# Causal attention with decay and an MLP mixer: scores computed a second time in transposed layout, with the maximum as an operand row

## The chip, the cores and the metric

The kernel runs on one core of a Trainium2 chip. The metric is the device time of one execution in microseconds. Before: median of 3 runs 1118.24 us (1116.69 to 1120.88).

## The reference

8 batches of 8 heads, 576 positions, head dimension 64. The outputs of all heads of a batch, 576 x 512, then go through a token mixing and a channel mixing layer, with a residual in each.

```python
scores = scale * np.matmul(q, k.transpose(0, 1, 3, 2))
log_f = np.log(np.clip(f, 0.0001, 1.0))
cum = np.cumsum(log_f, axis=-1)
decay = cum[:, :, :, None] - cum[:, :, None, :]
scores = np.where(causal, -1000000000.0, scores + decay)
scores = scores - np.max(scores, axis=-1, keepdims=True)
attn = np.exp(scores)
attn = attn / (np.sum(attn, axis=-1, keepdims=True) + 1e-09)
x = np.matmul(attn, v)          # then laid out as batch, position, head * dimension
xt = x.transpose(0, 2, 1)
h = np.maximum(xt @ w_tok1, 0.0) @ w_tok2
u = x + h.transpose(0, 2, 1)
h2 = np.maximum(u @ w_ch1, 0.0) @ w_ch2
return u + h2
```

The weights come in as doubles and are decoded on the chip. Nearly every product is made from two parts: a number is written as hi + lo, both fp32r, and hi x hi, hi x lo and lo x hi are added up in PSUM.

## The kernel before, in words

`build` walks through the 64 heads and records every operation with its engine, duration, reads, writes, buffers and a priority; `Plan.run` then places them, always the ready operation with the lowest priority whose buffers are free, and this fixes the order on each engine's queue. The priority is the head's number plus offsets from tables (`OFF`, `STEP`, `HEAD` and others). All DMAs stand on SyncE's queue, in that order.

A head, in tiles of queries with 64, 128, 128, 128, 128 rows (t = 0 to 4). For a pair of heads q and k are loaded into `raw` and split into `hl` (hi on GpSimd, lo on GpSimd); three gathers of 288 KB each (line 834) bring hi and lo of one head into the operands `k1` and `k2`, and two small DMAs bring the cumulated decay into rows of `k2`. `score` (line 861) multiplies in two passes, `k1` and `k2`, queries on the PSUM partitions; `rmin` (868, VectorE) adds the mask and takes the minimum of the negated row; `expo` (875, ScalarE) writes the exponentials to SBUF (`pr`) and their sums, which a second instruction reads out; lines 893 and 896 form the reciprocal; `norm` (903, GpSimd) multiplies the five tiles. Then 15 transposes of 128 x 128 (917, TensorE, fp32) bring the probabilities to keys on partitions, ScalarE and VectorE copy them out as hi and lo (585, 594), GpSimd moves a lo part (588), and the values are the weights of up to 512 moving columns of probabilities (lines 987 to 999): 11 matmuls, the result with dimensions on partitions. ScalarE and VectorE add hi and lo sums into `xt` (1037, 1044, 1047). Heads 0 to 3 (`FQ`, `FV`) skip the splitting: they multiply fp32 data directly.

After 4 and after 8 heads of a batch, `mixer` runs for half of the channels: `trx` transposes x (1416, 10 transposes), `tok1` and `tok2` mix the tokens, 28 matmuls of 256 and 24 of 288 columns; `tok2` adds the residual on VectorE (1487). After the second half `ch1` and `ch2` do two of twelve blocks of the channel layer (96 matmuls of 288 columns). u and the partial sums go to HBM.

When all heads are done, the attention buffers are given up for the other channel weights. Two chunks of 512 positions are done with 10 blocks of the channel layer (480 matmuls of 512 columns), seven with a Strassen scheme (per chunk 210 of 256 and 120 of 512 columns). Before the first score TensorE does 120 small filler matmuls (line 645), in early gaps.

```python
for of, j0, w in segs:
    for x, k in enumerate((at(k2),) if fq else (at(k1), at(k2))):
        nc.tensor.matmul(ps[:m, of : of + w], k[:, 0, i0 : i0 + m], k[:, 1, j0 : j0 + w], start=(x == 0), stop=(fq or x == 1))
...
def tr(out, i, j, pr=pr):
    nc.tensor.transpose(out, at(pr)[:, poff[i] + start[j] : poff[i] + end[j]], E["ident"])
```

Of the kernel before, what the change touches and what calls it, by code (L numbers as in the profile page):

```python
# [15 lines left out]
P = 128  # L16

PRM = dict(
    FILL=120, EP=3, DB=0, DLAST=1, F1=2, FQ=4, FV=4, LAG=3.88, n_raw=1, n_vr=2, n_hl=1, n_k1=2, n_k2=2, n_vv=2,
    E_hi='POOL', E_lo='POOL', E_vh='ACT', E_vl='POOL', E_nrm='POOL', n_pr=3, n_p34=2, n_p2=2, n_p1=1, n_p0=1, n_low=1,  # L20
    n_ring=12, n_part=4, n_xt=2, n_d_raw=3, n_d_g=2, n_hid=3, DEC3=11.96, SPREAD=10.59, SPREADA=6.46,
)
OFF = dict(
    load=-19.94, kh=41.36, kl=82.19, qh=-131.14, ql=-77.18, vh=-106.52, vl=134.93, s4=5.08, s3=5.41, s2=-18.34, mn=9.94,
    ex=6.58, rec=-18.92, nrm=-207.34, t3=4.41, t2=-99.36, t1=-68.13, t0=-31.7, hl=-31.09, av=4.12, fold=-29.94,
    fpe=3.65, lo0=-43.16, fev=-183.41, u=-72.11, dec=73.32, dec2=37.66, dec3=1.32, cd=-18.17, vload=-19.23,
)
# [516 lines left out]
def build(nc, env, dims):  # L544
# [61 lines left out]
    def decay():  # L606
# [6 lines left out]
        def c():  # L613
            return asf(at(cc)[:, 2, :])
# [1141 lines left out]
```

## Time and profile before

| | |
|---|---|
| median of the runs | 1118.24 us |
| the profiled execution | 1112.94 us |
| its span | 1111.2 us |
| busy: TensorE, VectorE, ScalarE, GpSimd | 1069.8, 765.0, 644.0, 546.4 us |
| mean granted clock | 0.991 |
| scores, from the first to the last start (L861) | 13.2 to 585.4 us |

Start and length of a matmul are given in the profile; the length holds the way through the array and overlaps the next, so the distance between two starts in an unbroken row is what one costs. Weight loads (PEld) are instructions of their own beside the matmuls. An fp32 matmul that is not a transpose shows as two records.

### The profile page before, as it was taken

Reading aid. Unit: us, or ns where it says so; the run is one execution under the profiler, and the core shown is the slowest. Engines: PE = TensorE matmul, PEld = TensorE weight load, DVE = VectorE, ACT = ScalarE, POOL = GpSimd, SP = SyncE. Lnnn points to the kernel's source line nnn. Section 1 sums busy time; section 2 is a strip of 40 time slices with the busy share of each in tenths; the row PEclk is TensorE's granted clock in tenths of the full one; section 3 lists DMA queues with packets and bytes.
Section 4 is the critical chain, followed back from the end, with each engine's and each line's share of the span. In section 5 each row is a group of like instructions: output and inputs, shape, how many; then the busy total and the mean of one; then the engine's idle time right before and its main releaser. Section 6 shows DMA issues by size and latency. Waiting matters only on the chain.

```text
span 1111.2 us, 20873 instructions
## 1 busy us (share of the span) xinstructions
PE 1069.8 (96%) x7172; PEld 962.4 (87%) x7172; DVE 765.0 (69%) x1944; ACT 644.0 (58%) x1657; POOL 546.4 (49%) x631
## 2 busy tenths in 40 slices
PE   8998979999999999999999999999999999999998
PEld 5577868999899999889898888889989898989896
DVE  6787878788787777778788896566455554637362
ACT  5776767778788777778776543244242433424241
POOL 5576876778678676777763305703123030303010
PEclk9999999999999999999999999999999999999999
DMA  8577675876777686767762544231212121212011
GB/s 225 144 176 165 158 201 142 217 215 174 202 179 206 177 194 194 185 193 176 181 171 82 184 145 125 68 113 40 76 39 77 38 77 39 76 39 76 16 62 39
DMA packets 69610, 146.79 MB, mean 132 GB/s; under 512 B 9424, under 2 KB 26832, under 8 KB 68480
## 3 DMA queue, kind: packets, MB, share of 16 engines
q1 hardware_dynamic: 69504, 145.45, 47.8%
q8 instruction: 57, 0.93, 0.4%
q14 instruction: 49, 0.40, 0.1%
HBM read 63.46 MB, written 28.31 MB: 83 GB/s over the span
## 4 chain that ended last, share of the span: by engine, by line
PE 75%; DMA 9%; DVE 6%; SPq 3%; ACT 3%; POOL 2%; issue 2%; DVEq 0%; POOLq 0%; ACTq 0%
DMA k<-hl 8%; PE bank L917 6%; PE pair L1364 6%; PE pair L1363 6%; PE pair L1365 6%; PE bank L861 6%; PE bank L1300 5%; PE bank L1302 5%; PE bank L1301 5%; PE pair L861 2%; PE pair L997 2%; PE pair L999 2%; SPq L834 2%; PE bank L1130 2%; PE pair L1151 2%
## 5 line engine op out<-in xcount | busy, mean ns | idle before, releaser
L903 POOL TENSOR_SCALAR pr<-pr,rec 128x576 f32<-128x576 f32 (+4 forms) x320 | 165.9, 539 | 53.9 <-DVE rec L896 33.1
L1334 POOL TENSOR_TENSOR part<-part,xt 128x512 f32<-128x512 f32 x28 | 36.0, 1316 | 277.3 <-DMA part<-pd 205.0
L585 ACT ACTIVATE p<-bank 128x384 fp32r<-128x384 f32 (+3 forms) x300 | 128.4, 474 | 45.2 <-PE bank L917 41.8
L917 PE MATMUL bank<-ident,pr 128*128 128x128 f32 (+1 forms) x960 | 137.9, 277 | 5.7 <-DVE p L594 2.0
L875 ACT ACTIVATE pr<-bank,nmin 128x448 f32<-128x448 f32 (+3 forms) x256 | 118.0, 467 | 36.9 <-DVE nmin L868 35.0
L594 DVE TENSOR_TENSOR p<-bank,p 128x384 fp32r<-128x384 f32 (+1 forms) x180 | 106.4, 595 | 41.0 <-ACT p L585 39.2
L1310 DVE TENSOR_TENSOR dd<-bank,dd 128x256 f32<-128x256 f32 x245 | 98.0, 422 | 52.3 <-PE bank L1302 50.3
L868 DVE CUSTOM_DVE_ANT_0 bank<-bank,mask 128x448 f32<-128x448 f32 (+3 forms) x256 | 107.0, 433 | 29.7 <-PE bank L861 26.1
L917 PEld LDWEIGHTS bank<-ident,pr 128*128 128x128 f32 (+1 forms) x960 | 109.3, 132 | 19.2 <-DVE low L594 3.4
L1363 PE MATMUL pair<-hid,w2r 128*128 128x512 f32 x280 | 109.0, 389 | 0.0
L1364 PE MATMUL pair<-hid,w2r 128*128 128x512 f32 x280 | 109.0, 389 | 0.0
L1365 PE MATMUL pair<-hid,w2r 128*128 128x512 f32 x280 | 108.9, 389 | 0.0
L594 DVE TENSOR_TENSOR hid<-dd,hid 128x512 fp32r<-128x512 f32 x70 | 48.4, 692 | 86.3 <-ACT hid L585 86.3
L861 PE MATMUL bank<-k 128*128 128x320 f32 (+1 forms) x480 | 88.9, 310 | 10.1 <-DMA k<-hl 8.4
L585 ACT ACTIVATE hid<-dd 128x512 fp32r<-128x512 f32 x70 | 44.0, 629 | 89.9 <-PE pair L1364 89.0
L1313 ACT ACTIVATE dd<-dd 128x256 f32<-128x256 f32 x140 | 56.8, 415 | 61.4 <-DVE dd L1310 59.2
L1300 PE MATMUL bank<-ring,w1r 128*128 128x256 f32 x280 | 79.8, 285 | 0.1
L861 PEld LDWEIGHTS bank<-k 128*128 128x128 f32 (+1 forms) x480 | 64.0, 178 | 18.2 <-DMA k<-hl 8.5
L1302 PE MATMUL bank<-ring,w1r 128*128 128x256 f32 x280 | 79.1, 283 | 0.0
L1301 PE MATMUL bank<-ring,w1r 128*128 128x256 f32 x280 | 79.1, 282 | 0.0
L999 PE MATMUL pair<-p,vv 128*128 128x512 f32 x240 | 75.6, 323 | 0.0
L790 POOL TENSOR_TENSOR hl<-raw,hl 128x1152 fp32r<-128x1152 f32 x27 | 72.5, 2684 | 1.8
(152 smaller groups left out, 3250.3 us busy)
## 6 DMA issues: line engine op xcount, KB each, us to landing
k<-hl SPq DMA_DIRECT2D x180, 288.0 KB
raw<-in_qk SPq DMA_DIRECT2D x30, 576.0 KB
vr<-in_v SPq DMA_DIRECT2D x32, 320.0 KB
ud<-xt SPq DMA_DIRECT2D x8, 1152.0 KB
pd<-part SPq DMA_DIRECT2D x32, 288.0 KB
out_t<-part SPq DMA_DIRECT2D x36, 256.0 KB
dd<-in_w_ch SPq DMA_DIRECT2D x12, 512.0 KB
dd<-in_w_ch SPq DMA_DIRECT2D x40, 128.0 KB
```

The lines of the kernel that those rows point to most:

```text
L585: nc.scalar.activation(out, in_, func, scale=scale)
L594: nc.vector.tensor_tensor(out, in_, asf(hi), op=ALU.subtract)
L861: nc.tensor.matmul(ps[:m, of : of + w], k[:, 0, i0 : i0 + m], k[:, 1, j0 : j0 + w], start=(x == 0), stop=(fq or x == 1))
L875: nc.scalar.activation(at(pr)[:m, poff[t] : poff[t] + w], at(buf)[:m, of : of + w], AF.Exp, bias=E["nmin"][sm][:m, t : t + 1], scale=-1.0, ...
L903: nc.gpsimd.tensor_scalar(x, x, r, 0.0, op0=ALU.mult, op1=ALU.add)
L917: nc.tensor.transpose(out, at(pr)[:, poff[i] + start[j] : poff[i] + end[j]], E["ident"])
L1300: nc.tensor.matmul(q, wh[:, cs], h_, start=c == 0, stop=False)
L1301: nc.tensor.matmul(q, wl[:, cs], h_, start=False, stop=False)
L1302: nc.tensor.matmul(q, wh[:, cs], l_, start=False, stop=c == 1)
L1363: nc.tensor.matmul(q, wh, h_, start=x == 0, stop=False)
L1364: nc.tensor.matmul(q, wl, h_, start=False, stop=False)
L1365: nc.tensor.matmul(q, wh, l_, start=False, stop=x == F2 - 1)
```

## The change

Scores are multiplied twice. First, with the hi parts only, queries on partitions (`ascore`, five tiles in six matmuls): VectorE takes the maximum of each row (`mx`). A transpose of the five columns of maxima, a ScalarE copy with factor -1 (`mt`) and a DMA of 2560 bytes put them as a row into `k2` (`md`). Then the scores are multiplied again in both terms with keys on the partitions (`bscore`), the maximum being subtracted by that row. ScalarE takes the exponential in place in PSUM, VectorE clamps what lies beyond the diagonal by a minimum with `tri`, and hi and lo parts are copied to `pp`. There is no normalizing before the values, and no transpose of probabilities.

The probabilities are now the weights, 128 (for the last tile 64) columns, and v is the moving operand: lo, hi and two columns of ones in 130 columns for the hi part, 66 for the lo part, so that the sum of a row comes out as a column. 15 pairs of tiles, two matmuls each, with tokens on the partitions. ScalarE and VectorE add the two sums, GpSimd multiplies by the reciprocal (`nx`), and hi and lo parts go to `xn`, which `tok1` reads; `trx` is gone. In `tok2` the residual is added on TensorE by matmuls with `xn` as weights and an identity as moving operand (11 for each of 4 channel blocks and batch), and ScalarE copies the result out, where VectorE added before. The fp32 path of the first four heads is gone. `k2` has three buffers, not two. Priorities come from a table `PR` with a value for each single operation, in place of the offsets; the plan's other rules are as before.

```diff
-    FILL=120, EP=3, DB=0, DLAST=1, F1=2, FQ=4, FV=4, LAG=3.88, n_raw=1, n_vr=2, n_hl=1, n_k1=2, n_k2=2, n_vv=2,
+    FILL=120, EP=3, DB=0, F1=2, n_raw=1, n_vr=1, n_hl=1, n_k1=2, n_k2=3, n_vv=2, n_pp=5, n_tm=1, n_xs=2, n_mt=3,
...
+            pr_("kh", n), lambda k2=k2, f=gather: f(at(k2)[0:D, T0:].rearrange("p (a s) -> p a s", a=2), 0, 2),
+        dma(pr_("kl", n), lambda k1=k1, f=gather: f(at(k1)[0:D], 0, 3), 294912, dur=650, rate=220, rd=[(hl, 0), (hl, 1)], wr=[(k1, 0)], bufs=[k1, hl])
+        dma(pr_("kl", n, 0.01), lambda k1=k1, f=gather: f(at(k1)[D:P], 1, 2), 294912, dur=650, rate=220, rd=[(hl, 0), (hl, 1)], wr=[(k1, 1)], bufs=[k1, hl])
...
+        def ascore(t, where=where, k2=k2):
+            buf, segs = where[t]
+            i0 = T0 + end[t] - P
+            for of, j0, w in segs:
+                nc.tensor.matmul(at(buf)[:, of : of + w], at(k2)[: D + 2, i0 : i0 + P], at(k2)[: D + 2, PADQ + j0 : PADQ + j0 + w], start=True, stop=True)
...
+            nc.vector.tensor_tensor_reduce(x, x, E["mask"][:, S - w : S], 1.0, -3e38, op0=ALU.add, op1=ALU.max, accum_out=E["mx"][sm][:, t : t + 1])
...
+            "PE", [tp_(P, NS)], pr_("mt", n), lambda um=um, sm=sm: nc.tensor.transpose(at(um)[:NS, :P], E["mx"][sm], E["ident"]),
...
+        dma(pr_("md", n), lambda mt=mt, k2=k2: nc.sync.dma_start(asf(at(k2)[D + 2 : D + 3, :PADQ]), asf(at(mt))), 2560, dur=650, rd=[mt, "rows"], wr=[(k2, "m")], bufs=[mt, k2])
...
+            def bscore(u=u, ps=ps, k1=k1, k2=k2):
+                segs = [(512 - HS, 0, 0, HS), (512, 0, HS, HS)] if u == "c" else [(of, j, kst[j], kw[j]) for j, of in UNITS[u]]
+                for of, j, q0, w in segs:
+                    o_, a, m = at(ps)[: ksz[j], of : of + w], kst[j], ksz[j]
+                    nc.tensor.matmul(o_, at(k1)[:, 1, a : a + m], at(k1)[:, 0, q0 : q0 + w], start=True, stop=False)
+                    nc.tensor.matmul(o_, at(k2)[: D + 3, PADQ + a : PADQ + a + m], at(k2)[: D + 3, T0 + q0 : T0 + q0 + w], start=False, stop=True)
...
+            p.op("ACT", d_act(w_), pr_("ex" + u, n), lambda f=region: nc.scalar.activation(f(), f(), AF.Exp, scale=1.0 / D**0.5), wr=[ps], bufs=[ps])
...
+                nc.vector.tensor_tensor(x, x, y, op=ALU.min)
...
+            p.op("ACT", d_act(w_), pr_("hi" + u, n), lambda f=region, pb=pb, w_=w_: hi_act(at(pb)[:, 0, :w_], f()), rd=[ps], wr=[(pb, 0)], bufs=[ps, pb])
+            p.op("DVE", d_dve(w_), pr_("lo" + u, n), lambda f=region, pb=pb, w_=w_: lo_dve(at(pb)[:, 1, :w_], f(), at(pb)[:, 0, :w_]), rd=[ps, (pb, 0)], wr=[(pb, 1)], bufs=[ps, pb])
...
+        def avt(ts, av=av, vv=vv, v0=v0, pp=pp):
+            for t in ts:
+                m = ksz[t]
+                for j in range(t + 1):
+                    u, of = AT_[j]
+                    c0 = of + P * (t - j)
+                    for z in (0, 1):
+                        w = at(pp[u])[: ksz[j], z, c0 : c0 + m]
+                        a, c = (T0, 2 * D + 2) if z else (0, 2 * D + 2)
+                        nc.tensor.matmul(
+                            at(av)[:m, AVS * t + a : AVS * t + c], w, at(vv)[: ksz[j], v0 + j, a:c], start=(j == 0 and z == 0), stop=(j == t and z == 1)
+                        )
...
+        p.op(ENG["ev"], d_act(NS * D), pr_("ev", n), lambda A=A, tm=tm: hi_on(ENG["ev"], at(tm), A()[:, :, 0:D]), rd=avs, wr=[tm], bufs=[av, tm])
...
+        p.op("DVE", d_dve(NS * D), pr_("xs", n), lambda A=A, tm=tm, xs=xs: nc.vector.tensor_tensor(at(xs), A()[:, :, D : 2 * D], at(tm), op=ALU.add), rd=[*avs, tm], wr=[xs], bufs=[av, tm, xs])
+        p.op("POOL", d_ptt(NS * D), pr_("nx", n), lambda xs=xs, sm=sm: nc.gpsimd.tensor_tensor(at(xs), at(xs), rec(sm).unsqueeze(2).to_broadcast([P, NS, D]), op=ALU.mult), rd=[("rec", sm)], wr=[xs], bufs=[xs])
...
+        p.op(ENG["xh"], d_hi(ENG["xh"], NS * D), pr_("xh", n), lambda xn=xn, xs=xs, hc=hc: hi_on(ENG["xh"], at(xn)[:, :NS, hc], at(xs)), rd=[xs], wr=[(xn, h, 0)], bufs=[xn, xs])
+        p.op("POOL", d_ptt((NS - 1) * D), pr_("xl", n), lambda xn=xn, xs=xs, hc=hc: lo_pool(at(xn)[:, NS:, hc], at(xs)[:, : NS - 1], at(xn)[:, : NS - 1, hc]), rd=[xs, (xn, h, 0)], wr=[(xn, h, 1)], bufs=[xn, xs])
...
-            def trs(ps=ps, blocks=blocks, w=w, first=g == (2,), tr=tr):
-                for x, (i, j) in enumerate(blocks):
-                    tr(at(ps)[:, x * P : (x + 1) * P], i, j)
...
-        def norm(t, sm=sm, pr=pr):
-            m = size[t]
-            x = at(pr)[:m, poff[t] : poff[t] + end[t]]
...
-        def av0(av=av, vv=vv, v0=v0, pb=p0_, fv=fv, vr=vr):
-            x, w_, r_ = (at(av)[:D], at(vr)[:T0, v0, :], at(pb)[:T0]) if fv else (at(av), at(vv)[:, v0, :], at(pb))
-            nc.tensor.matmul(x[:, 512:1024], w_, r_[:, T0:], start=True, stop=False)
-            nc.tensor.matmul(x[:, off : off + T0], w_, r_[:, :T0], start=True, stop=True)
...
-        def avj(seq, pb, av=av, vv=vv, v0=v0, fv=fv, vr=vr):
-            for j, c0, z in seq:
-                w, last = S - start[j], (j, z) == (3, 0)
-                x = at(av)[:, off + start[j] : off + S]
-                if fv:
-                    nc.tensor.matmul(x[:D], at(vr)[:, v0 + j, :], at(pb)[:, c0 : c0 + w], start=False, stop=last)
-                elif z:
-                    nc.tensor.matmul(x[:D], at(vv)[:, v0 + j, :D], at(pb)[:, 1, c0 : c0 + w], start=False, stop=last)
-                else:
-                    nc.tensor.matmul(x, at(vv)[:, v0 + j, :], at(pb)[:, 0, c0 : c0 + w], start=False, stop=last)
-
...
-    def trx(g):
...
-                            at(ps)[:m, i * W + c * P : i * W + (c + 1) * P], at(xt)[:, part * HC + c, start[t] : end[t]], E["ident"]
...
+                    if k == NT - 1:
+                        for t, z, a, e_ in own_x:
+                            eye = E["eyes"] if t == NS - 1 else E["eye"][:, a - t * P : e_ - t * P]
+                            nc.tensor.matmul(at(ps)[:, a - hf * HS : e_ - hf * HS], at(xn)[:, t + NS * z, ds], eye, start=False, stop=False)
```

In the middle of the attention stage, on TensorE, stood before: transposes of probabilities (`pr`) between scores (`k`) and values (`p`, `vv`).

```order
L917 MATMUL bank_68<-ident,pr_156 128x128 x4
L861 MATMUL bank_66<-k_149 128x320
L861 MATMUL bank_66<-k_151 128x320
L861 MATMUL bank_66<-k_149 128x192
L861 MATMUL bank_66<-k_151 128x192
L917 MATMUL bank_65<-ident,pr_156 64x128 x4
L997 MATMUL pair_64<-p_159,vv_152 64x384
L999 MATMUL pair_64<-p_159,vv_152 128x384
```

Now it reads, at a like place, with `pp` the probabilities and `vv` the values:

```order
L761 MATMUL pair_64<-vv_165,pp_170 128x130
L761 MATMUL pair_64<-vv_165,pp_170 128x66
L761 MATMUL pair_64<-vv_165,pp_167 128x130
L761 MATMUL pair_64<-vv_165,pp_167 128x66
L761 MATMUL pair_64<-vv_165,pp_167 128x130
L761 MATMUL pair_64<-vv_165,pp_167 128x66
L761 MATMUL pair_64<-vv_165,pp_168 64x130
L761 MATMUL pair_64<-vv_165,pp_168 64x66
L761 MATMUL pair_64<-vv_165,pp_170 64x130
L761 MATMUL pair_64<-vv_165,pp_170 64x66
L761 MATMUL pair_64<-vv_165,pp_167 64x130
L761 MATMUL pair_64<-vv_165,pp_167 64x66
```

The transposes are gone, and each value matmul has weights of its own and few columns.

In `tok2` one block of the mixer stood on TensorE as six matmuls:

```order
L1473 MATMUL bank_67<-held,ring_129 128x288
L1474 MATMUL bank_67<-held,ring_129 128x288
L1475 MATMUL bank_67<-held,ring_130 128x288
L1473 MATMUL bank_67<-held,ring_129 128x288
L1474 MATMUL bank_67<-held,ring_129 128x288
L1475 MATMUL bank_67<-held,ring_130 128x288
```

Now, with `x` the split outputs and `eye` the identity:

```order
L1177 MATMUL bank_65<-held,ring_134 128x288
L1182 MATMUL bank_65<-held,ring_134 128x288
L1183 MATMUL bank_65<-held,ring_135 128x288
L1177 MATMUL bank_65<-held,ring_134 128x288
L1181 MATMUL bank_65<-eye,x_133 128x128 x4
L1181 MATMUL bank_65<-eye,x_133 128x32 x2
L1182 MATMUL bank_65<-held,ring_134 128x288
L1183 MATMUL bank_65<-held,ring_135 128x288
```

Six matmuls with new weights stand among them.

On SyncE, in the middle of the attention stage, before, with `hl` the split inputs, `cc` the decay, `ud` the store of u:

```order
L810 DMA vr_146<-in_v 128x640
L828 DMA k_151<-cc_164 2x1x576 x2
L834 DMA k_148<-hl_147 64x2x576
L834 DMA k_148<-hl_147 64x1152
L834 DMA k_151<-hl_147 64x2x576
L1498 DMA ud_102<-xt_122 128x2304
L828 DMA k_150<-cc_164 2x1x576 x2
L810 DMA vr_145<-in_v 128x640
```

Now, with `mt` the maxima:

```order
L658 DMA k_160<-cc_175 2x1x576
L664 DMA k_158<-hl_156 64x2x576
L664 DMA k_158<-hl_156 64x1152
L710 DMA k_161<-mt_162 1x5x128
L1210 DMA ud_112<-x_132 128x2304
L710 DMA k_159<-mt_162 1x5x128
L664 DMA k_160<-hl_156 64x2x576
L664 DMA k_161<-hl_156 64x2x576
L658 DMA k_161<-cc_175 2x1x576
L664 DMA k_157<-hl_156 64x2x576
```

The transfer of the maxima stands in order with the gathers and the stores.

More of the change, by code (lines that the diff above doesn't have):

```diff
@@ L552, in build @@
     end = [a + b for a, b in zip(start, size)]
-    poff = [sum(end[:t]) for t in range(NS)]
     F2 = NF - F1
     p = Plan()
-    LAG, FQ, FV = PRM["LAG"], PRM["FQ"], PRM["FV"]
     def mm_(n, m=P):
@@ L719, in go @@
             def go(prio):
-                if t == 0:
-                    loads = [(sl(r * T0, T0), sl(0, DT), w_tok1[0:T0, :]) for r in (0, 1)]
+                if t == NS - 1:
+                    loads = [(sl(r * T0, T0), sl(0, DT), w_tok1[P * t :, :]) for r in (0, 1)]
                 else:
-                    loads = [(full, sl(0, DT), w_tok1[start[t] : end[t], :])]
+                    loads = [(full, sl(0, DT), w_tok1[P * t : P * t + P, :])]
                 decode(prio, loads, DT, lambda: E["t1h"][:, t, :], lambda: E["t1l"][:, t, :], ("t1", t))
@@ L907, in build @@
-        p.op("DVE", 72, n + o["rec"], rec1, rd=[("sums", sm, t) for t in range(NS)], wr=[("rec", sm)])
-        p.op("DVE", 100, n + o["rec"], rec2, wr=[("rec", sm)])
-        for t in (4, 3, 2, 1, 0):
-            p.op(ENG_NRM, d_pts(end[t], 1) if ENG_NRM == "POOL" else d_dve(end[t], True), n + o["nrm"], lambda t=t, f=norm: f(t), rd=[("rec", sm)], wr=[(pr, t)], bufs=[pr])
-        p34, p2_, p1_, p0_ = (Buf(("f" if fv else "p") + x) for x in ("34", "2", "1", "0"))
-        low = Buf("low")
-        def tr(out, i, j, pr=pr):
-            nc.tensor.transpose(out, at(pr)[:, poff[i] + start[j] : poff[i] + end[j]], E["ident"])
@@ new lines, in A, with rec @@
+        def A(av=av):
+            return at(av)[:, : AVS * NS].rearrange("p (t c) -> p t c", t=NS)
+        def rec(r):
+            return E["rec"][r]
+        avs = [(av, x) for x in range(3)]
+        p.op(ENG["ev"], d_act(NS * D), pr_("ev", n), lambda A=A, tm=tm: hi_on(ENG["ev"], at(tm), A()[:, :, 0:D]), rd=avs, wr=[tm], bufs=[av, tm])
+        p.op("DVE", 76, pr_("rc", n), lambda A=A, sm=sm: nc.vector.tensor_scalar(rec(sm), A()[:, :, 2 * D], 1e-9, None, op0=ALU.add), rd=avs, wr=[("rec", sm)], bufs=[av])
@@ L1433, in mixer @@
+    if "u" not in st:
+        st["u"], st["xt"] = {}, Buf("ux")
+    u, xt = st["u"], st["xt"]
+    heads = [(xn, h, z) for h in range(part * H // 2, (part + 1) * H // 2) for z in range(3)]
     h1 = []
@@ L1635, in attn_mixer_kernel @@
     )
-    for nm, shape in (("nmin", [P, NS]), ("sums", [P, NS + 1]), ("rec", [P, NS // 2 + 1, 4])):
-        E[nm] = [const.tile(shape, F32, name=f"{nm}{i}") for i in range(4)]
-    for x in E["sums"]:
-        nc.vector.memset(x, 1.0)
+    tri = E["tri"] = const.tile([P, P + 64], F32, name="tri")
+    nc.gpsimd.memset(tri, 3e38)
+    for a, w in ((0, 64), (64, P)):
+        nc.gpsimd.affine_select(
+            out=tri[:, a : a + w], in_=tri[:, a : a + w], pattern=[[1, w]], compare_op=ALU.is_ge, fill=0.0, base=0, channel_multiplier=-1
+        )
+    eye = E["eye"] = const.tile([P, P], F32R, name="eye")
+    eyes = E["eyes"] = const.tile([P, 64], F32R, name="eyes")
+    nc.vector.tensor_copy(eye, ident)
+    for a in (0, 64):
+        nc.vector.tensor_copy(eyes[a : a + 64], ident[a : a + 64, a : a + 64])
+    for nm in ("mx", "rec"):
+        E[nm] = [const.tile([P, S // P + 1], F32, name=f"{nm}{i}") for i in range(4)]
+    for x in E["mx"]:
+        nc.vector.memset(x, 0.0)
+    for x in E["one"].values():
+        nc.vector.memset(x[64:, :64], 0.0)
+    nc.vector.memset(pairs[1][64:, 704:834], 0.0)
     E["lower"] = const.tile([P, 1], F32, name="lower")
```

749 lines of the change are left out of this document (322 added, 427 removed), and 192 rows, old and new, of tables (av, cd, ex, fold).

## Prediction

> **What bounds the kernel now.** I read the busy times and the chain on the page first, then busy times by stage.
>
> ```profile
> span 1111.2 us, 20873 instructions
> PE 1069.8 (96%) x7172; PEld 962.4 (87%) x7172; DVE 765.0 (69%) x1944; ACT 644.0 (58%) x1657; POOL 546.4 (49%) x631
> ...
> PE 75%; DMA 9%; DVE 6%; SPq 3%; ACT 3%; POOL 2%; issue 2%; DVEq 0%; POOLq 0%; ACTq 0%
> ```
>
> ```profile
> 0.00:200.00 200.00, 177.84 (x1243) 144.34 (x1244) 153.34 (x452) 139.62 (x384) 138.91 (x187) 0.97 0.69 175
> 200.00:650.00 450.00, 435.35 (x3223) 409.99 (x3222) 362.65 (x1003) 339.88 (x924) 300.05 (x359) 1.00 0.68 181
> 650.00:1111.00 461.00, 456.57 (x2710) 408.07 (x2708) 248.97 (x493) 164.54 (x351) 107.46 (x86) 1.00 0.20 65
> ```
>
> After 650 us TensorE alone is full (456.6 of 461) and nothing there is changed. Before it, attention, TensorE is nearly full, VectorE and ScalarE stand at 76 to 81%, and a quarter of the chain is not TensorE. The mean length of a matmul overlaps its neighbours, so I price matmuls by the distance from start to start. The rows, from one stretch of the attention stage, TensorE:
>
> ```profile
> 378.12 0.28 PE L1450 MATMUL bank<-ring,held 128*128 128x256 f32 x1
> 378.24 0.28 PE L1452 MATMUL bank<-ring,held 128*128 128x256 f32 x1
> ...
> 383.05 0.69 PE L861 MATMUL pair<-k 128*128 128x288 f32 x4
> 383.57 0.34 PE L997 MATMUL pair<-p,vv 128*64 128x384 f32 x1
> 383.75 0.34 PE L999 MATMUL pair<-p,vv 128*128 128x384 f32 x1
> 383.93 0.60 PE L917 MATMUL bank<-ident,pr 128*128 128x128 f32 x4
> 384.29 0.31 PE L999 MATMUL pair<-p,vv 128*128 128x128 f32 x1
> 384.43 0.34 PE L997 MATMUL pair<-p,vv 128*64 128x128 f32 x2
> 384.61 0.28 PE L999 MATMUL pair<-p,vv 128*128 128x256 f32 x1
> 384.73 1.18 PE L861 MATMUL bank<-k 128*128 128x320 f32 x8
> 385.74 0.30 PE L1449 MATMUL bank<-ring,held 128*128 128x256 f32 x1
> ```
>
> 256 columns cost 0.12 us, 288 cost 0.13 (0.52 for four), 384 cost 0.18, 128 and 256 together 0.18, so 0.06 for 128. That is 0.42 ns a column and some 10 ns. The chain gives the rest: 512 columns (5.7% of 1111.2 us over 280 matmuls: 0.226 us), eight transposes in 0.87 us (0.109 each), and the fp32 matmuls of heads 0 to 3, two records each.
>
> ```profile
> by line: DMA k<-hl 8.2%; PE bank L917 5.7%; PE pair L1364 5.7%; PE pair L1363 5.7%; PE pair L1365 5.7%; PE bank L861 5.7%; PE bank L1300 5.3%; PE bank L1302 5.2%; PE bank L1301 5.2%; PE pair L861 2.4%; PE pair L997 2.0%; PE pair L999 1.9%;
> ...
> 0.75 2.97 DMA xt<-in_f
> ...
> 13.25 2.31 PE bank L861 x8
> ...
> 24.58 2.07 PE bank L861 x8
> 26.65 0.97 PE pair L861 x4
> ...
> 37.64 1.00 PE pair L987 x2
> ...
> 39.31 1.00 PE pair L995 x2
> ...
> 41.49 0.79 PE pair L995 x2
> 42.87 0.79 PE pair L995 x4
> ...
> 240.43 0.87 PE bank L917 x8
> ...
> 374.66 6.42 DMA k<-hl
> ```
>
> Now TensorE's work per head. A pass of scores has 1600 columns: 0.25 for 320 and 192 (1.01 us hold two heads' two passes), 0.20 for 448, 0.05 for 64, 0.26 for two of 288, and 0.03 between groups: 0.79. Two passes 1.58, fifteen transposes 1.64, values 1.43 (three of 512, two each of 384, 256 and 128, one of 64): 4.65, times 60 heads 279. Heads 0 to 3 cost 3.04 + 1.64 + 3.58 = 8.26 each: 33. Sum 312. The mixers have per batch 20 transposes, 56 matmuls of 256 and 144 of 288 columns: 2.2 + 6.7 + 19.2 = 28.1, times 8 is 225. Fillers 15, the channel stage 1320 matmuls of 512 and 1470 of 256: 298 + 176. In all 1026. The span holds 1111, 13 of it before the first score and 4 after the last matmul, so some 68 us are waits of TensorE, all before 650 us.
>
> **The change part by part.** Its price hangs on the weight loads. Every value matmul now has the probabilities as weights, 130 or 66 moving columns, and 128 (or for the last token tile 64) weight columns. The loads of the same stretch:
>
> ```profile
> 384.26 0.19 PEld L999 LDWEIGHTS pair<-p,vv 128*128 128x128 f32 x1
> 384.37 0.20 PEld L997 LDWEIGHTS pair<-p,vv 128*64 128x64 f32 x2
> 384.49 0.19 PEld L999 LDWEIGHTS pair<-p,vv 128*128 128x128 f32 x1
> ```
>
> A load of 128 columns frees the loader 0.11 us later, two of 64 in 0.12. The same is seen among the scores of 192 columns, one stretch further, where the matmul needs only 0.09 us:
>
> ```profile
> 385.02 0.19 PEld L861 LDWEIGHTS bank<-k 68*128 68x128 f32 x1
> ...
> 385.13 0.30 PEld L861 LDWEIGHTS bank<-k 128*128 128x128 f32 x2
> ...
> 385.25 0.34 PEld L861 LDWEIGHTS bank<-k 68*128 68x128 f32 x2
> ```
>
> Again 0.11 and 0.12 between loads. So I take 0.108 us as the floor of a matmul with 128 new fp32r weight columns and 0.058 with 64; in the kernel before it hides under 256 columns and more. The Trainium skill, "TensorE: Matmul & The Clock Gate", section "LDWEIGHTS (loading the stationary operand)", states the columns divided by 1.2 GHz, 107 ns for 128: the trace agrees with 0.11.
>
> Values: 15 pairs of token tile and key tile, hi and lo, 30 matmuls a head: 20 x 0.108 + 10 x 0.058 = 2.74, some 2.70 with the first loads hidden, against 1.43. By the columns alone (20 x 0.061 and 0.031 in pairs) it would be about 1.5. Transposes of probabilities: 1.64 fall away, one transpose of maxima (0.11) comes. Scores: the first pass has 1600 columns once, 0.79 and 0.03 more because its 64 columns now stand behind 128 weight columns; the second has two terms, 1.62. A head then costs 0.82 + 0.11 + 1.62 + 2.70 = 5.25 us, for all 64 (the fp32 path of heads 0 to 3 goes): 336, against 312. So +24.
>
> Mixers: 160 transposes of x go, 17.4 us. The residual comes as 352 matmuls with an identity as moving operand (11 in each of 32 channel blocks), each with 128 new weight columns: 352 x 0.108 = 38. So +21. TensorE's work grows by 45 us.
>
> Start: 13.25 us to the first score now, straight from the fp32 inputs. Then the input must be split and gathered first: 6.4 us for a gather (its row above) against the 3.5 that the first score waits now; I add 6, between 3 and 10.
>
> What becomes lighter is beside TensorE:
>
> ```profile
> L903 POOL TENSOR_SCALAR pr<-pr,rec 128x576 f32<-128x576 f32 (+4 forms) x320 | 165.9, 539 | 53.9 <-DVE rec L896 33.1
> ...
> L588 POOL TENSOR_SCALAR p<-low 64x576 fp32r<-64x576 f32 x60 | 41.0, 683 | 40.3 <-DVE low L594 34.8 <-ACT ring L585 1.0 <-DVE rec L893 1.0
> ...
> L875 ACT ACTIVATION_READ_ACCUMULATOR pr<-bank,nmin 128x1 f32 x192 | 38.3, 199 | 0.0
> ...
> L1334 POOL TENSOR_TENSOR part<-part,xt 128x512 f32<-128x512 f32 x28 | 36.0, 1316 | 277.3 <-DMA part<-pd 205.0
> ```
>
> GpSimd loses 207 us and gets some 120 (three products or differences a head, 320, 256 and 64 columns at the 2.6 ns a column of L1334). ScalarE loses the reading of 320 sums, 64 us, and two of five exponentials a head; the copy of the mixer's result moves to it. VectorE loses the splitting of x and that add, and gets three clampings of the diagonal a head: roughly even. Together with a longer stage they stand at 60 to 75% instead of 76 to 81%. So of the 68 us of waits I let half go, 34: the gathers and the single buffer of split inputs are as before, and the first 200 us still hold the decoding of weights. The bounds are none and all.
>
> What is added as a wait: a head's maxima go over TensorE, a ScalarE copy and a DMA of 2.5 KB into the operand before the second scores can start. No such transfer stands in the trace; its nearest rows are 2.97 us (a lone load at the start) and 6.42 us (a gather among others), and with issue and copies the trip takes 4.5 to 8 us. On SyncE it stands in order with the gathers and the 1152 KB stores, so what is queued behind it are the next heads' gathers. (SyncE's other issues change little: one decay row transfer a head less, one for V a pair more.) I take it as covered, because three operand buffers rotate at a period of some 10 us a head: filling (6.4), first scores and five maxima (4.5), the trip (up to 8) and the second scores (up to 6) make 25 of 30 us.
>
> Sum: 1111 + 45 + 6 - 34 = 1128 us of span. The profiled execution took 1112.94 us with a span of 1111.2, and the median of the runs is 1118.24, 5.3 above it. So 1128 + 1.7 + 5.3 = 1135 us.
>
> **The rivals.**
>
> Waits go altogether (faster or equal). For it: every engine but TensorE loses load, and priorities are now set for each single operation. Against: the waits sit mostly where the gathers and decoding are, and these stay. If 55 to 68 us go instead of 34, the time is 1101 to 1114. It decides from 40 us on.
>
> The loads hide after all (faster). If a load of 128 columns took what a matmul of 128 takes, 0.06, values would cost 1.6 a head and the identities 20 us: 70 + 18 less, TensorE's work 43 below now, and with all waits kept about 1081. Against it stand the gaps of 0.11 to 0.12 above, all of fp32r weights. The Trainium skill has a rule by which it would be so, in the same page's section "Weight-path perf modes — Fast Weight Load (FWL) and DoubleRow": a fast weight load is on when 128 weights are loaded and their type is not FP32. By that rule the time would be this rival's; the trace shows no such load for fp32r.
>
> The maxima's trip is not covered (slower still). It decides from the point where filling, first scores, trip and second scores together pass 30 us. Half a microsecond a head beyond it is 32 us on TensorE's queue, a whole one 64: 1167 to 1199. For it: the trip can queue behind gathers of 6.4 us; against it, the 5 us left in the sum above.
>
> That the work is not what it says I give no chance: each instruction stands in the order.
>
> **How the numbers follow.** The sum 0.50 (1118 to 1158), all waits gone 0.20, loads hidden 0.12, the trip exposed 0.18. A measurement here cannot tell less than about 0.5%, 5.6 us, from no change. Faster than 1112.6: most of the second and all of the third, 0.27. Within 1112.6 to 1123.8: the rest of the second and the lower end of the first, 0.15. Slower: 0.58. The range leaves out most of the hidden loads and the upper part of the exposed trip: 1095 to 1178.
>
> **What would show it.** Right: value matmuls at 0.108 us start to start, the last head's values some 45 us of work later than now, TensorE's share of the chain above 75%, GpSimd near 460 us busy. Wrong: value loads 0.06 apart; second scores waiting for the DMA into k in most heads; or waits of TensorE under 20 us.

## The result, and the profile after

The changed kernel takes 1253.52 us (median of 4 runs, 1245.93 to 1263.31), the kernel before 1117.63 (1116.69 to 1120.88, 4 runs): the ratio is 1.12, 95% interval 1.113 to 1.13. That is 136 us slower. I had forecast slower, but by 17 us, and 1253 lies far outside the range of 1095 to 1178. The profiled execution took 1256.27 us with a span of 1254.2, 143 us above the span before. A run over 1.5% above the fastest of its kernel counts as slow and stands outside the ranges given below; of the traces shown, that of cols66 is of such a run.

The page of the changed kernel, busy times, the granted clock in 40 slices (a digit is a tenth of full speed), and the chain by engine:

```profile
span 1254.2 us, 21978 instructions
...
PE 1203.7 (96%) x8124; PEld 1113.3 (89%) x8124; DVE 744.7 (59%) x1917; ACT 588.7 (47%) x1235; POOL 466.1 (37%) x455
...
PEclk8767798897999989999969669999999999999999
...
PE 86%; DVE 6%; ACT 2%; DMA 2%; issue 2%; POOL 1%; SPq 0%; DVEq 0%; ACTq 0%; POOLq 0%
```

The same clock row of the kernel before:

```profile
PEclk9999999999999999999999999999999999999999
```

Much is as forecast: GpSimd stands at 466 us (near 460 was expected), TensorE has 86% of the chain, 96% of its time is busy. New is the clock row: through the whole attention stage, which now ends near 760 us, its digits are 6 to 9. The busy times by stage of the changed kernel (span, then busy time and count of TensorE, its weight loads, VectorE, ScalarE, GpSimd, then the granted clock, the DMA share and GB/s):

```profile
0.00:200.00 200.00, 181.96 (x1310) 169.31 (x1311) 129.58 (x399) 104.74 (x217) 102.27 (x119) 0.80 0.66 167
200.00:650.00 450.00, 432.31 (x3316) 415.17 (x3315) 271.83 (x840) 253.96 (x536) 215.61 (x211) 0.92 0.62 154
650.00:760.00 110.00, 102.67 (x663) 98.47 (x662) 60.62 (x148) 50.31 (x106) 34.13 (x35) 0.78 0.37 99
760.00:1254.00 494.00, 486.75 (x2844) 430.37 (x2842) 282.71 (x532) 179.73 (x378) 114.06 (x90) 1.00 0.22 72
```

Before, the first two stretches had 0.97 and 1.00. A busy share of 96% hides this: a matmul at half clock takes nearly twice as long (rows below), and counts as busy all the time.

**How to split the 143 us.** Span times one minus the mean granted clock is the most that the clock can have taken away. Before: 1111.2 x (1 - 0.991) = 10 us. After: 1254.2 x (1 - 0.922) = 98 us. So 88 of the 143 us are clock, and 55 are left at full clock (1101 and 1156 us). A second split, from the distance between every two matmul starts in the traces, with a gap counted as a wait where it is over 150 ns longer than columns or load need (300 at half clock): work at full clock 1045 before and 1100 after (+55), lost to half clock 11 and 91 (+80), waits 49 and 57 (+8). Both say the same: about 55 us of work, some 80 to 88 of clock, hardly any change in waits.

**What half clock does to a head.** Two rows from the timeline of the changed kernel, TensorE: first a whole head's 30 value matmuls at half clock with the matmul behind them, then the same at full clock.

```profile
67.71 5.52 PE L761 MATMUL pair<-vv,pp 128*128 128x130 f32 x30
73.16 0.53 PE L723 MATMUL bank<-k 128*128 128x192 f32 x1
...
715.07 3.04 PE L761 MATMUL pair<-vv,pp 128*128 128x130 f32 x30
718.04 0.39 PE L1153 MATMUL bank<-xn,held 128*128 128x256 f32 x1
```

From start to start 2.97 us at full clock (2.70 was my figure) and 5.45 at half. These matmuls go by their weight loads, so the loads slow down too.

**How it falls and comes back.** The trace's record of the granted clock knows two values, 1 and 0.5, in steps of 3.41 us. Between 20 us and the end of the attention stage it falls 5 times before and 10 times after; but before, each fall lasts one step (5 steps in all), after, they add up to 55 steps. One fall of each kernel, by windows, first before, then after:

```profile
467.40:470.80 3.40, 2.08 (x14) 1.81 (x14) 2.73 (x11) 2.46 (x6) 3.29 (x7) 1.00 1.00 268
470.80:474.30 3.50, 3.15 (x14) 2.88 (x15) 3.34 (x8) 2.47 (x8) 3.33 (x4) 0.51 0.20 42
474.30:477.70 3.40, 3.40 (x31) 3.28 (x29) 2.19 (x8) 3.22 (x9) 3.40 (x3) 1.00 0.61 173
```

```profile
457.50:460.90 3.40, 2.30 (x17) 1.86 (x16) 3.40 (x13) 1.88 (x4) 1.53 (x3) 1.00 1.01 204
460.90:474.60 13.70, 13.18 (x64) 12.51 (x64) 5.66 (x19) 5.46 (x12) 7.28 (x7) 0.50 0.45 111
686.20:689.60 3.40, 1.79 (x15) 1.59 (x15) 2.71 (x13) 1.29 (x2) 0.48 (x2) 1.00 0.65 172
689.60:713.50 23.90, 23.41 (x112) 22.66 (x112) 9.18 (x26) 9.27 (x20) 3.53 (x6) 0.50 0.23 63
```

In these three falls a step with much waiting (TensorE busy 1.8 to 2.3 of 3.4 us) is followed by half clock, in both kernels. Before, one busy step brings the clock back. After, it stays at half for four and seven steps though TensorE is busy all along.

### The profile page after: what moved, and what is told of

It is laid out like the page before. It is cut to its first block, busy times and chain, and to the rows that moved or that the text cites. A ratio compares the mean times of both kernels' runs of the same rounds, so it can differ in the third digit from the quotient of the medians.

```text
span 1254.2 us, 21978 instructions
## 1 busy us (share of the span) xinstructions
PE 1203.7 (96%) x8124; PEld 1113.3 (89%) x8124; DVE 744.7 (59%) x1917; ACT 588.7 (47%) x1235; POOL 466.1 (37%) x455
## 4 chain that ended last, share of the span: by engine, by line
PE 86%; DVE 6%; ACT 2%; DMA 2%; issue 2%; POOL 1%; SPq 0%; DVEq 0%; ACTq 0%; POOLq 0%
PE pair L761 16%; PE pair L1102 5%; PE pair L1101 5%; PE pair L1100 5%; PE bank L1037 5%; PE bank L1038 5%; PE bank L1039 5%; PE bank L1181 3%; PE bank L723 3%; PE bank L686 3%; PE bank L724 2%; PE bank L1153 2%; PE bank L1182 2%; PE bank L1154 2%; PE bank L1177 2%
## 5 line engine op out<-in xcount | busy, mean ns | idle before, releaser
L761 PEld LDWEIGHTS pair<-vv,pp 128*128 128x128 f32 (+2 forms) x1920 | 228.2, 198 | 6.4 <-ACT ring L405 0.5
L761 PE MATMUL pair<-vv,pp 128*128 128x130 f32 (+5 forms) x1920 | 233.4, 280 | 0.4 <-DVE xs L783 0.2
L1071 POOL TENSOR_TENSOR part<-part,x 128x512 f32<-128x512 f32 x28 | 35.3, 1292 | 251.4 <-DMA part<-pd 214.0
L784 POOL TENSOR_TENSOR xs<-xs,rec 128x320 f32<-128x320 f32 x64 | 47.0, 734 | 210.2 <-DVE xs L783 131.7
L414 DVE TENSOR_TENSOR pp<-bank,pp 128x512 fp32r<-128x512 f32 x128 | 86.6, 686 | 14.2 <-ACT pp L405 13.2
L734 ACT ACTIVATE bank<-bank 128x512 f32<-128x512 f32 x128 | 73.8, 582 | 26.2 <-PE bank L724 24.1
L724 PE MATMUL bank<-k 67*64 67x64 f32 (+3 forms) x256 | 80.6, 321 | 0.0
L405 ACT ACTIVATE pp<-bank 128x512 fp32r<-128x512 f32 x128 | 74.7, 596 | 11.9 <-DVE bank L744 10.6
L723 PE MATMUL bank<-k 128*64 128x64 f32 (+3 forms) x256 | 79.5, 347 | 0.7 <-ACT mt L600 0.6
L411 POOL TENSOR_TENSOR ring<-x,ring 128x576 fp32r<-128x576 f32 (+1 forms) x40 | 58.0, 1457 | 55.8 <-ACT ring L405 49.6
```

The source lines that it names most:

```text
L405: nc.scalar.activation(out, in_, func, scale=scale)
L414: nc.vector.tensor_tensor(out, in_, asf(hi), op=ALU.subtract)
L723: nc.tensor.matmul(o_, at(k1)[:, 1, a : a + m], at(k1)[:, 0, q0 : q0 + w], start=True, stop=False)
L724: nc.tensor.matmul(o_, at(k2)[: D + 3, PADQ + a : PADQ + a + m], at(k2)[: D + 3, T0 + q0 : T0 + q0 + w], start=False, stop=True)
L761: nc.tensor.matmul(at(av)[:m, AVS * t + a : AVS * t + c], w, at(vv)[: ksz[j], v0 + j, a:c], start=(j == 0 and z == 0), stop=(j == t and z ...
```

## The experiments

**Theory A**: the clock follows the share of each 3.41 us step in which columns stream through the array; time spent on loading weights counts as little as waiting. The value matmuls stream few columns under each load: 15 pairs with 196 columns at 0.417 ns (from start to start 256 columns take 0.120 us and 512 take 0.227) are 1.23 us of 2.97, a share of 0.41 (0.365 where both loads have 128 columns). So a short wait throws the clock to half, and at half clock (a share of 0.45) they can't bring it back. **Theory B**: waits alone decide it. **Theory C**: too much work lowers the clock. Besides these: where the 55 us of work are, and why waits did not fall.

### The clock by itself

```diff
+for n in (192, 144, 130, 120, 112, 104, 98, 88, 80, 64):
+    warm()          # 200 matmuls of 256 columns
+    down(n)         # 200 of n columns, each with 128 new weight columns
...
+for n in (160, 180, 200, 208, 216, 224, 232, 240, 256):
+    up(n)           # 100 of 32 columns, then 150 of n
```

> Leaves out the whole computation: only stretches of back-to-back fp32r matmuls, each with 128 new weight columns and N moving columns, without any wait. First stretches of 200 with N = 192, 144, 130, 120, 112, 104, 98, 88, 80 and 64, a stretch of 256 columns ahead of each; then nine stretches of 100 with N = 32, each followed by 150 with N = 160, 180, 200, 208, 216, 224, 232, 240, 256. Theory A (the clock follows the share of a 3.41 us window in which columns stream through the array; it falls below about 0.41 and rises above about 0.86): at full clock a matmul takes 0.112 us by its load, so the clock should stay full down to N = 112 (0.42) and fall to half in the stretches of N = 98 (0.36) and fewer; at half clock a load takes 0.213 us, so after N = 32 it should stay half for N = 160 to 208 (up to 0.81) and come back for N = 224 (0.88) and more. Theory B (the clock falls only where TensorE waits): it stays full in all stretches. Theory C (it falls with too much work, as a limit on power would): it falls in the stretches with most columns.

Windows inside the stretches of 112, 104 and 98 columns, then inside those of 160, 180 and 200 behind 32 (nothing else runs, so only TensorE and its loads are busy):

```profile
218.00:238.00 20.00, 20.00 (x181) 20.00 (x181) 0.00 (x0) 0.00 (x0) 0.00 (x0) 1.00 0.00 1
264.00:284.00 20.00, 20.00 (x181) 20.00 (x181) 0.00 (x0) 0.00 (x0) 0.00 (x0) 1.00 0.01 2
314.00:347.00 33.00, 33.00 (x157) 33.00 (x156) 0.00 (x0) 0.00 (x0) 0.00 (x0) 0.50 0.00 0
582.00:612.00 30.00, 30.00 (x143) 30.00 (x142) 0.00 (x0) 0.00 (x0) 0.00 (x0) 0.50 0.00 1
640.00:665.00 25.00, 25.00 (x119) 25.00 (x119) 0.00 (x0) 0.00 (x0) 0.00 (x0) 0.50 0.00 1
696.00:706.00 10.00, 10.00 (x92) 10.00 (x91) 0.00 (x0) 0.00 (x0) 0.00 (x0) 1.00 0.00 0
```

At full clock a matmul with a new load takes 20 / 181 = 0.1105 us, with 112 columns as with 104. 104 columns (share 0.39) hold the clock, 98 (0.37) lose it, as do all smaller counts. At half clock a load takes 0.21 us; 160 columns (0.64) and 180 (0.71) leave it at half, 200 (0.79) and all above bring it back within 5.5 us. Theory A holds, with the upper bound somewhat lower than the 0.86 that I had read from the kernel; B and C are out for bare matmuls: TensorE never waits here, and the clock falls where there is least to compute. The Trainium skill, "TensorE: Matmul & The Clock Gate", section "What's actually happening", tells of such a gate, half or full by how busy the array has been, with a window of 3413 ns: the trace agrees with its 3.41 us. The Trainium skill, same page, section "HAM oscillation — how this bites in real kernels", gives as the rule that no idle gap over some 3.4 us may come; here the clock falls with no gap at all, and the measurement decides.

```diff
+for n, k in ((256, 28), (256, 12), (256, 8), (256, 5), (160, 28), (160, 18), (160, 12), (160, 8), (120, 28), (120, 12)):
+    warm()
+    bursts(n, k, 128, 16 if k > 12 else 24)   # k matmuls, then a wait for two ScalarE copies
```

> Leaves out the whole computation: bursts of fp32r matmuls with 128 new weight columns, and after each burst a wait for two small ScalarE copies, some 0.9 us by the latencies of the changed kernel's trace. Ahead of each series 200 matmuls of 256 columns. Theory A (share of the window in which columns stream, waits counting as nothing streamed; it falls under about 0.375): 256 columns in bursts of 28, 12, 8 and 5 give 0.71, 0.55, 0.46 and 0.36, so only the last falls; 160 columns in bursts of 28, 18, 12 and 8 give 0.46, 0.42, 0.36 and 0.30, the last two fall; 120 columns, which held the clock without waits (0.45), fall with bursts of 28 (0.35) and 12. Theory B (a wait of a given length makes it fall, whatever runs around it): all series alike.

From the last start of a burst to the next start it took some 0.7 us, not 0.9, so all shares are higher than I had put them. Windows inside the series of 256 columns by 5, 160 by 28, 160 by 12 and 160 by 8:

```profile
274.00:295.00 21.00, 17.36 (x62) 13.82 (x62) 0.00 (x0) 4.42 (x24) 0.00 (x0) 0.50 0.00 0
340.00:378.00 38.00, 33.94 (x286) 32.39 (x285) 0.00 (x0) 3.68 (x20) 0.00 (x0) 1.00 0.00 1
...
487.00:527.00 40.00, 33.57 (x258) 30.12 (x256) 0.00 (x0) 8.10 (x44) 0.00 (x0) 1.00 0.00 1
564.00:600.00 36.00, 31.43 (x127) 28.21 (x128) 0.00 (x0) 5.53 (x30) 0.00 (x0) 0.50 0.00 0
```

256 columns held in bursts of 28, 12 and 8 and lost the clock in bursts of 5; 160 held by 28 and fell by 8; against the forecast, they held by 12 (258 x 160 x 0.417 ns in 40 us: 0.43) and fell by 18, there in one step that held two waits (share 0.38 in that step); 120 columns, which hold by themselves, fell with both bursts. The same wait does nothing among dense matmuls and throws the clock among thin ones, against B. Step by step the bound was 0.38 in both bare runs. In the full kernels it is less sharp: worked out from the matmuls' starts, the steps ahead of the changed kernel's ten falls have 0.25 to 0.41, but in cols240 (below) 0.48 was followed by a fall and 0.36 was not, and at half clock steps of up to 0.86 passed in the changed kernel before the clock came back.

### The kernel with other widths of the value matmuls

All four at the order and the loads of the changed kernel.

```diff
-                        a, c = (T0, 2 * D + 2) if z else (0, 2 * D + 2)
+                        a, c = (0, 2 * D + 2) if j == 0 and z == 0 else (T0, 2 * D + 2)     # cols66
+                        a, c = 0, 2 * D + 2                                                 # lo130
...
```

> The hi part of the probabilities, too, multiplies 66 columns (the first matmul of a tile still 130), so v's lo part is left out but for the first key tile: 10 of 30 value matmuls of a head lose 64 columns. Same order, same loads, less arithmetic. Theory A (columns streamed decide the clock): the value matmuls stream about 0.28 of the time, not 0.36, more windows fall under 0.37 and the clock comes back later: span times (1 - granted clock) rises from 98 to about 130 us, time about 1280 us (1262 to 1300). Theory B (waits alone): 1253 us or a few less.

> The lo part of the probabilities multiplies all 130 columns of v, not 66: 64 more columns in 960 matmuls, same order, same loads. Theory A (the clock follows the columns streamed): the value matmuls stream 0.48 of the time at full clock, not 0.36; those falls of the clock that come at shares of 0.35 to 0.40 (4 of 11) go, and some come back sooner: the loss to half clock falls from 91 to about 55 us, time about 1215 us. Theory B (it follows the waits alone): 1253 us, within 6. Theory C (more columns cost clock): over 1260 us.

```diff
...
+                        if t < NS - 1:                                                      # cols240
+                            g = 160 if t == 2 else 240
+                            o_ = at(av)[:m, AVS * t : AVS * t + g]
+                            r_ = at(vv)[: ksz[j], v0 + j : v0 + j + 2, :].rearrange("p a c -> p (a c)")[:, :g]
...
+                        if t != 2:                                                          # cols260
+                            o_ = at(av)[:m, AVS * t : AVS * t + 2 * c].rearrange("p (x c) -> p x c", x=2)
+                            r_ = r_.unsqueeze(1).to_broadcast([ksz[j], 2, c])
...
```

> Both parts of the probabilities multiply 130 columns, and for token tiles 0, 1, 3 and 4 a second time into columns that are not yet used: 260 moving columns in 24 of 30 value matmuls of a head, 130 in the others; same order, same loads. It does about three times the columns of the changed kernel. Theory A: those matmuls cost 0.121 us, not 0.112 (some 14 us in all), but stream 0.9 of the time at either clock, so the clock should do as in the kernel before: 10 to 20 us lost at half clock in place of 91, time about 1190 us (1175 to 1210). Theory B: 1253 + 14 = 1267 us. Theory C: over 1280 us.

> As the run with 260 columns, but without its two costs: 240 contiguous columns (100 ns of streaming under a load of 108) for token tiles 0, 1 and 3, 160 for tile 2, and 130 for tile 4, whose loads have 64 columns. Same order, same loads. Theory A (columns streamed decide the clock, falling under 0.37 to 0.39 and rising over 0.70 to 0.78 of a window, as the bare stretches showed): the value matmuls stay at 0.112 us, work grows by some 5 us, half clock costs about 45 us in place of 91, time 1213 us (1195 to 1230). Theory B (waits alone decide it): 1258 us.

A head's 30 value matmuls at full clock, in the timelines of cols66 and of cols240:

```profile
269.61 3.10 PE L761 MATMUL pair<-vv,pp 128*128 128x130 f32 x30
272.64 0.39 PE L1153 MATMUL bank<-xn,held 128*128 128x256 f32 x1
```

```profile
227.90 3.16 PE L766 MATMUL pair<-vv,pp 128*128 128x240 f32 x30
230.99 0.40 PE L1180 MATMUL bank<-held,ring 128*128 128x288 f32 x1
```

3.03 and 3.09 us, beside 2.97: the loads set it, the columns don't. What the columns do is hold the clock:

```profile
core 0: 1227.7 us, clock 0.968
```

That is cols240; the changed kernel has 0.922. All of them, with the time split as above:

| run | columns a head | time | clock part: span x (1 - clock) | rest: span x clock |
|---|---|---|---|---|
| cols66 | 2300 | 1278 to 1289 us (three runs) | 1277.1 x 0.103 = 132 us | 1146 |
| the changed kernel | 2940 | 1253.5 | 1254.2 x 0.078 = 98 | 1156 |
| lo130 | 3900 | 1251.3 | 1245.5 x 0.068 = 85 | 1161 |
| cols240 | 5620 | 1228.1 | 1227.7 x 0.032 = 39 | 1188 |
| cols260 | 7020 | 1275.6 | 1280.1 x 0.039 = 50 | 1230 |

The row of cols66 goes by its run of 1278.8 us, the others by the profiled run. Over three runs of cols66 and four of each other kernel the clock part is 126 to 136, 78 to 105, 80 to 96, 38 to 45 and 38 to 50 us, in the order of the table, so lo130 can't be told from the changed kernel, and the other three can. Least arithmetic is slowest of the first four: cols66 computes less and loses 25 to 35 us, as theory A put it. cols240 computes nearly twice as many columns, throws nearly half of them away, and gains 25 us. By B and C there is nothing to gain there, so they fall. But A's sizes were off. lo130 gained 2 us where I expected 38, which is what B had forecast; its share at half clock would be some 0.60 (3900 columns in 5.45 us), still under 0.71, and I take this as the reason. cols260 lost 22 us: I had forgotten that the 10 loads of 64 columns a head take half as long, so that 260 columns cover them by far. Its 1920 value matmuls take 249 us at full clock (1920 times their mean distance), against 192 in the changed kernel and 206 expected. The time alone would fit B's 1267 us better than A; it is the clock part, down to 50, that speaks for A. And cols240 stays 15 us above its forecast: its work grew by 13 us, its waits by 12.

### Where the work is

```diff
-                            nc.tensor.matmul(at(ps)[:, a - hf * HS : e_ - hf * HS], at(xn)[:, t + NS * z, ds], eye, start=False, stop=False)
+                            pass                                                            # noid
...
-                    for z in (0, 1):
+                    for z in (0,):                                                          # hi_only
```

> The identity matmuls are left out, and so the residual of the token mixer is missing from the result; same order otherwise. If they cost their loads on TensorE's path: 352 x 0.108 = 38 us less, about 1215 us (the clock may add or take 15). If TensorE waits at these places anyway: less than 15 us.

> The lo part of the probabilities is not multiplied with v: 15 value matmuls a head in place of 30; everything else stays, the making of the lo parts too. It prices the weight loads of the values. If they stand on TensorE's path at 0.100 us on average (192 us for 1920): 96 us less work, and since 130 columns to each load stream 0.48 of the time, up to 50 us less at half clock: 1253 - 96 - (0 to 50) = 1107 to 1157 us. If the loads hide behind other engines' work: less than 30 us gained.

> The runs hi_only and cols240 in one: 15 value matmuls a head, the lo part of the probabilities left out, with 240 moving columns for token tiles 0, 1 and 3, 160 for tile 2 and 130 for tile 4. Theory A with its parts adding up: against hi_only (1164 us, of whose profiled span 91 us is lost to the clock) the work grows by some 3 us, waits by up to 10, and the loss falls to 35 to 50 us: 1130 us (1115 to 1145). Theory B, or if the gain of cols240 was one of order or chance: 1160 us or more.

noid: 1211.7 us, 42 less; the identities were priced at 38. Not all of the 42 is their price: by the starts, work falls by 35 us and the loss to half clock by 18, and waits grow by 10. hi_only: 1163.9 us, 90 less and just outside the 1107 to 1157 that I forecast. Its profiled run has a rest of 1172.5 x 0.922 = 1081 us, 75 less than 1156; by the starts, work falls by 86 us and waits grow by 13.

```profile
core 0: 1172.5 us, clock 0.922
```

So the value loads stand on TensorE's path, as the prediction said. The two parts did not add up: hi_240 came to 1157.6 us, not 1130, near the 1160 that stood for theory B or chance. Its clock part is 58 to 77 us over four runs, against 75 to 91 in hi_only, where 35 to 50 were expected. With 130 columns to a load the value matmuls stream about half of the time already, so the falls that are left may come from waits that more columns don't help; no run here shows that.

### Why the waits did not fall

```diff
-        dma(pr_("md", n), lambda mt=mt, k2=k2: nc.sync.dma_start(asf(at(k2)[D + 2 : D + 3, :PADQ]), asf(at(mt))), 2560, dur=650, rd=[mt, "rows"], wr=[(k2, "m")], bufs=[mt, k2])     # no_md
...
-lambda f=region, pb=pb, w_=w_: lo_dve(at(pb)[:, 1, :w_], f(), at(pb)[:, 0, :w_])
+lambda: None                                                                               # hi_nolo, on hi_only
...
+            nc.sync.dma_start(asf(out[:, :, :16]), asf(at(hl)[rows, 1:3, :16]))             # gather16
...
-        return (m / 2.4, n / 2.4 + min(13.0, 0.052 * n))
+        return (m / 1.2, n / 2.4 + min(13.0, 0.052 * n))                                   # load108
+        return (m / 4.8, n / 2.4 + min(13.0, 0.052 * n))                                   # load27
```

> The transfer of the maxima is left out, and the second scores don't wait for it: the row in the operand keeps its ones, so one constant is subtracted in place of the row's maximum. First scores, maxima, their transpose and copy stay. If the trip of the maxima is covered, as the trace of the changed kernel has it (6.5 us of TensorE's waits end with it): within 15 us of 1253. If it holds up the second scores by way of the order: 30 us or more gained.

> As the run hi_only, and VectorE does not make the lo parts of the probabilities either (they are not used there): 87 us less for VectorE, and each of a head's three PSUM buffers comes free some 0.7 us sooner. Same order. Against hi_only, 1164 us: if TensorE's waits come from the load on VectorE or from how long a bank is held, waits fall by 20 us or more and the clock rises: 1115 to 1140 us. If they come from elsewhere (gathers, the order, single buffers): 1154 to 1166 us.

> One of a head's three gathers brings 16 columns in place of 576 (the other columns of that operand half hold ones, so the second scores lack their lo x hi term): 8 KB in place of 288, a third of the gathered bytes gone. Same order. If the waits that did not fall, and with them the falls of the clock, come from the gathers and their queue: TensorE's waits (57 us) fall by 12 us or more, the falls of the clock become fewer, and the time is 1225 us or less. If they come from the order and from chains between the engines: 1253 us, within 12.

> One number of the planner: a load of m weight columns counts m / 1.2 ns (107 for 128), as measured, in place of m / 2.4; everything else as in the changed kernel, so only the order moves. If the waits of TensorE, and with them the falls of the clock, come from an order that was planned for loads of half the length: waits fall from 57 to about 35 us, the loss to half clock from 91 to about 60: about 1200 us. If the order is not at fault (the priorities were set with the shorter loads, and a new order is only another order): 1253 us, within 20.

> As load108, but the planner's load of m columns counts m / 4.8 ns, half as long as in the changed kernel and a quarter of the measured one. If the 85 us that load108 lost came from any new order (the priorities fit the one set of durations they were made with): 1270 to 1350 us here too. If longer loads in the plan were themselves the cause: 1253 us or less.

TensorE's longest waits, total, times and longest, in the kernel before and in the changed one:

```profile
PE bank L861 <- DMA k<-hl: 8.4, 9, 2.4
PE pair L987 <- POOL p L588: 3.6, 4, 1.7
PE pair L987 <- DVE xt L1044: 2.7, 2, 1.4
```

```profile
PE bank L686 <- DMA k<-hl: 7.7, 3, 3.7
PE pair L686 <- DVE pp L414: 6.1, 6, 2.0
PE pair L723 <- DVE mx L692: 6.0, 6, 2.4
PE bank L1177 <- DVE ring L417: 3.8, 3, 1.8
PE pair L724 <- DMA k<-mt: 2.9, 2, 2.4
```

In the changed kernel they are spread over many causes: a gather, a bank that VectorE hasn't given free (lo parts, maxima), the mixer's hidden layer, and only 2.9 us for the maxima's transfer. No single cure worked. no_md: 1283.0 us, slower by 29, which neither side of its forecast had: without that transfer the planner puts the queues in another order, so the run prices another order and not the transfer alone. hi_nolo: 1144 to 1155 us in three runs (hi_only 1158 to 1175), at or just below the bracket for "elsewhere" and far from the other one; waits stayed (71 and 68 us by the starts), so neither the load on VectorE nor how long it holds a bank sets most of them. gather16: 1258.1 us; a third of the gathered bytes makes no difference. load108: 1338.1 us, load27: 1362.0, slower both, whichever way the plan's load is changed. As I read it, the table of priorities fits the one set of durations; all three other orders tried are worse. The spans and clocks of load108 and of no_md, a line each:

```profile
core 0: 1334.5 us, clock 0.870
```

```profile
core 0: 1280.4 us, clock 0.911
```

Their rests are 1334.5 x 0.870 = 1161 us and 1280.4 x 0.911 = 1166 us, beside 1156: 76 of the 80 us that load108's span is longer, and 16 of no_md's 26, are clock again. By the starts, waits are longer by some 19 us in load108 and 12 in no_md. That waits in unlucky steps cost several times their own length would fit this, but the new order also moves the thin matmuls to other steps, and the two are not told apart. What exactly makes those waits in the changed kernel stays open.

## Why the prediction was wrong, point by point

- **Direction and mechanism of the work: right.** TensorE's work grows: +55 us by the starts, forecast +45. The loads of 128 columns do set the value matmuls (0.11 us, with 66 columns as with 240). A head's values take 2.97 us, not 2.70, some 17 us more in all; the identities 35 by the starts when they are left out, forecast 38.
- **The sum failed in a step that it did not have.** "256 columns cost 0.12 us, 288 cost 0.13" was taken from a stretch at full clock and used for all of the span. The clock stood in the quoted windows (0.97, 1.00, 1.00), and the sum put its loss at nothing more for the new matmuls, without giving a reason. In its place the runs show a granted clock that depends on the very term that I had worked out: a load of 0.108 us over 66 to 130 columns streams 0.36 to 0.41 of the time, and this is at the bound. It costs 80 to 88 us in the profiled run.
- **Waits: wrong.** "Of the 68 us of waits I let half go": by the starts they went from 49 to 57. The 68 were a remainder and too many, since the sum of 1026 misses some 20 us of work (1045 by the starts) and 11 us of half clock. VectorE fell from 69% to 59%, ScalarE from 58% to 47%, GpSimd from 49% to 37% of the span, and TensorE waited as before. That they followed the load of other engines was an assumption; hi_nolo and gather16 speak against it. The rival in which all waits go is out as well. In the sum this and the start are 36 us.
- **Start: wrong by its whole size.** +6 us were forecast; the first score starts at 13.5 us, before at 13.25. The first gather took 3.65 us there, not 6.4, about as long as the load that the first score waited for before (3.53), and the splitting ran beside the work on the decay ahead of it.
- **The maxima's trip: right.** TensorE waits 2.9 us for it in all, and 2.2 for the copy ahead of it; the rival with the exposed trip (1167 to 1199) would have come nearer to the time, but for a reason that did not happen. The rival of hidden loads is out: 30 matmuls in 2.97 us.

In all: work +10, clock +80, waits and start +36 make the 126 us between 1128 and 1254.

Of the versions tried none beats the kernel before. At full clock throughout, by the first split, the changed kernel would still stand near 1156 us of span against 1101.

## What to carry to other kernels

When a change gives TensorE many matmuls with new weights and few columns, work out the share of time in which columns stream, not only the time of a load: in the bare runs the clock fell below about 0.38, and from half it stayed there at 0.71 and came back at 0.79; in whole kernels falls came at up to 0.48. Read the granted clock by stage beside the busy times, since a busy TensorE at half clock looks full. Where loads set the pace anyway, columns up to the load's length cost little (3.09 us a head beside 2.97) and hold the clock. Here the operand order of the kernel before, in which the long side moves, was faster still.

## What the runs showed of the hardware

- The granted clock has two values, full and half, in steps of 3.41 us. It fell in bare stretches between a streamed share of 0.39 and 0.37 and came back from half between 0.71 and 0.79, without TensorE ever waiting.
- At half clock an fp32r weight load of 128 columns takes 0.21 us, at full clock 0.1105: the load slows down with the array. The Trainium skill, "TensorE: Matmul & The Clock Gate", section "LDWEIGHTS (loading the stationary operand)", gives a load's nanoseconds as its columns divided by 1.2, by which 128 columns are estimated at 107 ns: the trace agrees at full clock only.
- A moving operand that repeats the same 130 columns (260 in all) ran as 260 columns do: 0.12 us.
